# Idle matmuls at the start of a fused attention and softplus kernel: seven instead of ten, and fewer in the gaps behind them

## The chip, the core and the metric

The kernel runs on one core of a Trainium2 chip. Its engines are TensorE (PE; its weight loads are shown as PEld), VectorE (DVE), ScalarE (ACT), GpSimd (POOL) and SyncE (SP), whose queue issues nearly all DMA transfers. Each engine takes its own instructions strictly in the order in which they were written down; semaphores tie the engines together. The metric is device time in microseconds, the median of several runs.

## The reference

```python
# q, k, v: (8, 8, 576, 64); omega: (128, 64); w_in: (512, 2048); w_out: (2048, 512)
def phi(x):                       # of q * scale and of k * scale
    proj = einsum('bhsd,md->bhsm', x, omega)
    h = proj - sum(x * x, axis=-1, keepdims=True) / 2.0
    h = h - max(h, axis=-1, keepdims=True)
    return exp(h) / sqrt(m)
...
kv = einsum('bhsm,bhsd->bhmd', k_p, v)
z = sum(k_p, axis=2)
attn = einsum('bhsm,bhmd->bhsd', q_p, kv) / (einsum('bhsm,bhm->bhs', q_p, z)[..., None] + 1e-06)
...
h = x @ w_in                      # x: attn as (4608, 512)
g = maximum(h, 0.0) + log1p(exp(-abs(h)))
out = g @ w_out
```

## The kernel before

The work is cut by batch (8) and by "quads" of four heads (2 a batch). Tokens of a quad come in units: `xk` and `xq` are the loaded tiles of keys and queries, `k_0_2` in a tile's name is quad 0, unit 2. Only the first batch matters for what follows; its units hold 128 tokens each, so there are ten units of keys (five for each quad) and ten of queries.

One unit of keys goes this way. SP loads it (L463; queries L465). ACT squares its rows (L474) and DVE sums the squares (L481). PE projects it with omega (L491) into two PSUM banks, `ppk_..._0` and `ppk_..._1`, one for each half of the partitions. DVE takes the maxima out of both banks (L541) and folds them into a bias (L548, L553), and ACT writes the exponents (L561), which frees the banks. For keys PE then adds up keys times values into `kt` (L700). For queries (`ppq`, `smq`) PE turns the exponents (`tpq`, L803), multiplies them with the sums `kvs` (L816), and so on. `x` then goes through the feed-forward part: layer 1 into `h` (L1049 to L1051, three products of high and low parts), softplus on ACT and DVE (L1055 to L1072), layer 2 into `acc` (L1109 to L1111). In between ACT, DVE and POOL unpack the weights (`rawi`, `rawo` to `wi`, `wo`, L373 to L394), which are loaded as 16 pairs.

All of it is first written down as a list of works, each with its engines, a planned cost, the works that it comes after, and the buffers that it takes and gives. `in_order` plays this list through with planned clocks and so fixes the order on every engine. Eight PSUM banks (`at`, `h`, `acc`) are given out by it.

The change concerns idle matmuls: `fill` multiplies a 128x128 tile with itself into a PSUM bank that nobody reads. Ten stand in front of everything else (on `idle`, a tile of zeros that DVE sets first). After planning, `with_fill` walks through PE's works, and where the plan leaves PE idle before a work, it writes idle matmuls (on `ident`) into the gap, as many as the constants give:

```python
n = int((t - last - FILL) / 0.2135) if last is not None and t < until else 0
if last is not None and t < DENSE and w.take:
    n += 2
```

`t` is the planned start of the work, `last` the planned end of the one before on PE, `until` is 70 (planned us), and `w.take` says that the work takes a bank. The matmuls go into a bank that is planned to be free all that time, or else into the bank that the work itself takes. On the core they are ordinary matmuls: PE does them before it does the work behind them, whether or not the plan's gap is there.

Of the kernel before, what the change touches and what calls it, by code (L numbers as in the profile page):

```python
# [35 lines left out]
MARGIN = 0.0000  # L36
START = {"SP": 0.75, "ACT": 1.9, "PE": 4.6}
SLOW = 7.19
FILL = 0.3
DENSE = 12  # L40
PATIENCE = {"PE": 0.0000, "DVE": 0.00, "ACT": 0.1822, "POOL": 0.00, "SP": 3.0950}
LEAN = {"DVE": 0.2675, "POOL": 0.1608, "ACT": 0.00}
SPREAD = ((0, 10.51), (17, 12.01))
# [213 lines left out]
def with_fill(out, held, banks, until, emit):  # L257

    last, all_ = None, []
    for i, w in enumerate(out):  # L260
        if w.engine == "PE":
            t = w.end - w.cost
            n = int((t - last - FILL) / 0.2135) if last is not None and t < until else 0
            if last is not None and t < DENSE and w.take:
                n += 2
            names = [
                b for b in banks if all(x1 <= last and g < i or x0 >= t and f >= i for x0, x1, f, g in held.get(b, []))
            ] if n > 0 else []
            names = names or [box[key] for _, box, key in w.take if box[key] in banks]
            if names and n > 0:  # L270
                all_.append((emit, names[0], n))
            last = w.end
        all_.append(w)
    return all_
# [3 lines left out]
def favor_softplus_kernel(ctx, tc, q0, k0, qx, kx, tx, vv, om, wi, wo, out):  # L278
# [11 lines left out]
    at = ctx.enter_context(tc.tile_pool(name="at", bufs=1))  # L290
# [4 lines left out]
    def bank(name, tag):  # L295
        return ps.tile([P, 512], F32, name=name, tag=tag, bufs=1)

    idle = at.tile([P, P], F32, name="idle", tag="x.0", bufs=1)
# [1280 lines left out]
    def fill(tag, n, idle=ident):  # L1579
        t = bank("fill", tag)[:, :P]  # L1580
        for _ in range(n):
            nc.tensor.matmul(t, idle, idle, start=True, stop=True)  # L1582

    with tc.manual_schedule():
        fill("at.0", 10, idle)
        for w in with_fill(*in_order(works, room, AHEAD, MARGIN), room["any"], 70, fill):
            if isinstance(w, tuple):
                w[0](*w[1:])
                continue
            w.emit(w.engine) if len(w.on) > 1 else w.emit()  # L1590
# [99 lines left out]
```

## Time and profile before

| what | value |
|---|---|
| median of 3 runs | 1006.22 us (1006.0 to 1007.1) |
| the profiled execution, own time | 1006.46 us |
| its span, first to last instruction | 1004.7 us |
| busy: PE, DVE, ACT, POOL | 99%, 80%, 67%, 8% of the span |
| mean granted TensorE clock | 0.999 |
| idle matmuls on PE | 45 (10 on `idle`, 35 on `ident`) |

Times within the trace count from the first instruction of the span. Matmuls are pipelined and their ends are modelled, so two that follow each other overlap in a row's duration, and start times say more than ends. A float32 matmul of the idle kind, of L491 or of L700 is two passes, and a row counts passes (x20 is ten matmuls). An engine's idle time stands in brackets before an instruction, with what ended it.

### The profile page before, as it was taken

Reading aid. Unit: us, or ns where it says so; the run is one execution under the profiler, and the core shown is the slowest. Engines: PE = TensorE matmul, PEld = TensorE weight load, DVE = VectorE, ACT = ScalarE, POOL = GpSimd, SP = SyncE. Lnnn points to the kernel's source line nnn. Section 1 sums busy time; section 2 is a strip of 40 time slices with the busy share of each in tenths; the row PEclk is TensorE's granted clock in tenths of the full one; section 3 lists DMA queues with packets and bytes.
Section 4 is the critical chain, followed back from the end, with each engine's and each line's share of the span. In section 5 each row is a group of like instructions: output and inputs, shape, how many; then the busy total and the mean of one; then the engine's idle time right before and its main releaser. Section 6 shows DMA issues by size and latency. Waiting matters only on the chain.

```text
span 1004.7 us, 17142 instructions
## 1 busy us (share of the span) xinstructions
PE 992.0 (99%) x5753; PEld 807.7 (80%) x5753; DVE 805.4 (80%) x2194; ACT 673.7 (67%) x1629; POOL 79.8 (8%) x90
## 2 busy tenths in 40 slices
PE   9999999999999999999999999999999999999998
PEld 8888888787778787887878787878788778788886
DVE  6999997988868787888888897979889846998600
ACT  6999987757677675666675756756576555777600
POOL 0113211000001000100000000100010000001000
PEclk9999999999999999999999999999999999999999
DMA  9963444443252424442343335243534121000011
GB/s 346 373 242 118 146 151 122 134 117 94 96 149 95 134 93 132 137 114 82 115 120 126 91 95 152 95 132 94 133 117 112 64 79 42 1 1 1 1 53 32
DMA packets 64334, 113.81 MB, mean 113 GB/s; under 512 B 18268, under 2 KB 37112, under 8 KB 64248
## 3 DMA queue, kind: packets, MB, share of 16 engines
q1 hardware_dynamic: 64088, 112.60, 36.1%
q8 instruction: 46, 0.75, 0.3%
q14 instruction: 40, 0.33, 0.1%
q10 hardware_dynamic: 160, 0.13, 0.1%
HBM read 85.68 MB, written 27.03 MB: 112 GB/s over the span
## 4 chain that ended last, share of the span: by engine, by line
PE 87%; DVE 6%; ACT 4%; DMA 1%; issue 1%; POOL 0%; DVEq 0%; ACTq 0%; SPq 0%
PE acc L1109 13%; PE acc L1110 12%; PE acc L1111 12%; PE h L1049 10%; PE h L1050 9%; PE h L1051 9%; PE ppk L491 3%; PE kt L655 3%; PE xp L977 3%; PE pb L1384 2%; PE ppq L516 2%; PE pc L1384 2%; PE pa L1384 1%; DMA xq<-qx 1%; PE fill L1582 1%
## 5 line engine op out<-in xcount | busy, mean ns | idle before, releaser
L1109 PE MATMUL acc<-wo,gh 128*128 128x512 f32 x512 | 204.1, 399 | 0.0
L1110 PE MATMUL acc<-wo,gh 128*128 128x512 f32 x512 | 200.2, 391 | 0.0
L1111 PE MATMUL acc<-wo,gl 128*128 128x512 f32 x512 | 199.7, 390 | 0.0
L1049 PE MATMUL h<-xh,wi 128*128 128x512 f32 (+1 forms) x512 | 190.8, 373 | 1.9 <-DVE u L1064 1.1
L1050 PE MATMUL h<-xl,wi 128*128 128x512 f32 (+1 forms) x512 | 186.1, 364 | 0.0
L1051 PE MATMUL h<-xh,wi 128*128 128x512 f32 (+1 forms) x512 | 185.8, 363 | 0.0
L1055 ACT ACTIVATE u<-h 128x512 f32<-128x512 f32 (+1 forms) x128 | 70.1, 547 | 81.4 <-PE h L1051 79.2
L1109 PEld LDWEIGHTS acc<-wo,gh 128*128 128x128 f32 x512 | 96.2, 188 | 24.9 <-issue 6.8
L1049 PEld LDWEIGHTS h<-xh,wi 128*128 128x128 f32 x512 | 96.4, 188 | 23.4 <-DVE u L1064 3.9
L1111 PEld LDWEIGHTS acc<-wo,gl 128*128 128x128 f32 x512 | 96.1, 188 | 21.2 <-DVE gl L1204 0.4
L1110 PEld LDWEIGHTS acc<-wo,gh 128*128 128x128 f32 x512 | 96.5, 188 | 15.9
L1051 PEld LDWEIGHTS h<-xh,wi 128*128 128x128 f32 x512 | 96.4, 188 | 15.4
L1050 PEld LDWEIGHTS h<-xl,wi 128*128 128x128 f32 x512 | 96.6, 189 | 13.5
L1064 DVE SCALAR_TENSOR_TENSOR u<-h,u 128x512 f32<-128x512 f32 (+1 forms) x128 | 79.2, 619 | 32.7 <-ACT u L1061 31.5
L1068 ACT CAST gh<-u 128x512 fp32r<-128x512 f32 (+1 forms) x101 | 57.2, 566 | 46.0 <-PE acc L1110 29.1
L1072 DVE TENSOR_TENSOR gl<-u,gh 128x512 fp32r<-128x512 f32 (+1 forms) x106 | 68.7, 648 | 14.9 <-ACT gh L1068 13.1
L1061 ACT ACTIVATE u<-u 128x512 f32<-128x512 f32 (+1 forms) x128 | 74.2, 580 | 3.9
L1058 ACT ACTIVATE u<-u 128x512 f32<-128x512 f32 (+1 forms) x128 | 74.3, 581 | 3.2
L887 DVE CUSTOM_DVE_ANT_0 junk<-phq,zb 128x128 bf16<-128x128 f32 (+1 forms) x228 | 67.4, 296 | 7.0 <-ACT phq L561 0.4
L538 ACT ACTIVATE phq<-phq,smq 128x128 f32<-128x128 f32 x194 | 59.5, 389 | 10.1 <-DVE smq L553 10.1
L561 ACT ACTIVATE phk<-ppk,smk 128x128 f32<-128x128 f32 x230 | 63.6, 375 | 3.3 <-DVE smk L553 3.1
L541 DVE TENSOR_REDUCE smk<-ppk 128x4 f32<-128x512 f32 (+2 forms) x80 | 46.0, 595 | 24.5 <-PE ppk L491 24.5
(217 smaller groups left out, 1764.2 us busy)
## 6 DMA issues: line engine op xcount, KB each, us to landing
xk<-kx SPq DMA_DIRECT2D x28, 512.0 KB, 3.8
xq<-qx SPq DMA_DIRECT2D x28, 512.0 KB, 3.6
fdq<-flq SPq DMA_DIRECT2D x28, 512.0 KB, 2.8
qq<-fdq SPq DMA_DIRECT2D x112, 128.0 KB, 2.9
rawi<-wi SPq DMA_DIRECT2D x16, 512.0 KB, 6.7
rawo<-wo SPq DMA_DIRECT2D x16, 512.0 KB, 10.1
out<-o SPq DMA_DIRECT2D x32, 256.0 KB, 2.1
v<-vv SPq DMA_DIRECT2D x14, 576.0 KB, 3.7
```

The source lines that it names most:

```text
L887: nc.vector.tensor_tensor_reduce(jk[r, c % jk.shape[1]], ph[r, c], q.zb[r, h], 1.0, 1e-6, ALU.mult, ALU.add, dn[r, 0, c : c + 1])
L1049: nc.tensor.matmul(b["h"], wh, xh[:, cc, t], start=cc == 0, stop=False)
L1050: nc.tensor.matmul(b["h"], wh, xl[:, cc, t], start=False, stop=False)
L1051: nc.tensor.matmul(b["h"], wl, xh[:, cc, t], start=False, stop=cc == NCC - 1)
L1055: nc.scalar.activation(b["u"], b["h"], AF.Abs)
L1058: nc.scalar.activation(b["u"], b["u"], AF.Exp, scale=-1.0)
L1061: nc.scalar.activation(b["u"], b["u"], AF.Ln, bias=1.0)
L1064: nc.vector.scalar_tensor_tensor(b["u"], b["h"], 0.0, b["u"], ALU.max, ALU.add)
L1072: (nc.vector if e == "DVE" else nc.gpsimd).tensor_tensor(b["gl"], b["u"], b["gh"].bitcast(F32), ALU.subtract)
L1109: nc.tensor.matmul(dst, gh, w2[fc][:, 0, c], start=start, stop=False, **kw)
L1110: nc.tensor.matmul(dst, gh, w2[fc][:, 1, c], start=False, stop=False, **kw)
L1111: nc.tensor.matmul(dst, gl, w2[fc][:, 0, c], start=False, stop=stop, **kw)
```

## The change

Seven idle matmuls stand in front instead of ten; the two extra ones ahead of each early work that takes a bank are gone, with the constant `DENSE`; and a planned gap has to be 1.0 us longer than the matmuls put into it, where it was 0.3 us.

```diff
--- before.py
+++ after.py
@@ -36,8 +36,7 @@
 MARGIN = 0.0000
 START = {"SP": 0.75, "ACT": 1.9, "PE": 4.6}
 SLOW = 7.19
-FILL = 0.3
-DENSE = 12
+FILL = 1.0
 PATIENCE = {"PE": 0.0000, "DVE": 0.00, "ACT": 0.1822, "POOL": 0.00, "SP": 3.0950}
 LEAN = {"DVE": 0.2675, "POOL": 0.1608, "ACT": 0.00}
 SPREAD = ((0, 10.51), (17, 12.01))
@@ -261,8 +260,6 @@
         if w.engine == "PE":
             t = w.end - w.cost
             n = int((t - last - FILL) / 0.2135) if last is not None and t < until else 0
-            if last is not None and t < DENSE and w.take:
-                n += 2
             names = [
                 b for b in banks if all(x1 <= last and g < i or x0 >= t and f >= i for x0, x1, f, g in held.get(b, []))
             ] if n > 0 else []
@@ -1582,7 +1579,7 @@
             nc.tensor.matmul(t, idle, idle, start=True, stop=True)
 
     with tc.manual_schedule():
-        fill("at.0", 10, idle)
+        fill("at.0", 7, idle)
         for w in with_fill(*in_order(works, room, AHEAD, MARGIN), room["any"], 70, fill):
             if isinstance(w, tuple):
                 w[0](*w[1:])
```

The plan itself, and with it the order of all other instructions on every engine, is the same. Of the 45 idle matmuls 23 are left: 7 in front, 1 ahead of the fifth group of projections (6 before), none ahead of the second, third and fourth (1 each), the sixth (5) and the first `kt` (2), 15 near 61 us (18) and none near 72 us (1).

The start of PE's queue, before (`ppk` is written by the projection of a unit of keys, four matmuls a group):

```order
L1582 MATMUL fill<-idle 128x128 x10
L491 MATMUL ppk_0_0_0_115<-omf,xk_0_0_106 128x128
L491 MATMUL ppk_0_0_1_116<-omf,xk_0_0_106 128x128
L491 MATMUL ppk_0_0_0_115<-omf,xk_0_0_106 128x128
L491 MATMUL ppk_0_0_1_116<-omf,xk_0_0_106 128x128
L1582 MATMUL fill<-ident 128x128
L491 MATMUL ppk_1_0_0_130<-omf,xk_1_0_108 128x128
L491 MATMUL ppk_1_0_1_131<-omf,xk_1_0_108 128x128
```

And in the changed kernel:

```order
L1579 MATMUL fill<-idle 128x128 x7
L488 MATMUL ppk_0_0_0_112<-omf,xk_0_0_103 128x128
L488 MATMUL ppk_0_0_1_113<-omf,xk_0_0_103 128x128
L488 MATMUL ppk_0_0_0_112<-omf,xk_0_0_103 128x128
L488 MATMUL ppk_0_0_1_113<-omf,xk_0_0_103 128x128
L488 MATMUL ppk_1_0_0_125<-omf,xk_1_0_105 128x128
L488 MATMUL ppk_1_0_1_126<-omf,xk_1_0_105 128x128
L488 MATMUL ppk_1_0_0_125<-omf,xk_1_0_105 128x128
```

Three idle matmuls fewer stand ahead of the first group, and none ahead of the second any more.

What PE does from the fourth group of projections (unit 1 of quad 1) on, before:

```order
L1582 MATMUL fill<-ident 128x128
L491 MATMUL ppk_1_1_0_159<-omf,xk_1_1_112 128x128
L491 MATMUL ppk_1_1_1_160<-omf,xk_1_1_112 128x128
L491 MATMUL ppk_1_1_0_159<-omf,xk_1_1_112 128x128
L491 MATMUL ppk_1_1_1_160<-omf,xk_1_1_112 128x128
L1582 MATMUL fill<-ident 128x128 x6
L491 MATMUL ppk_0_2_0_189<-omf,xk_0_2_123 128x128
L491 MATMUL ppk_0_2_1_190<-omf,xk_0_2_123 128x128
L491 MATMUL ppk_0_2_0_189<-omf,xk_0_2_123 128x128
L491 MATMUL ppk_0_2_1_190<-omf,xk_0_2_123 128x128
L1582 MATMUL fill<-ident 128x128 x5
L491 MATMUL ppk_1_2_0_216<-omf,xk_1_2_137 128x128
```

The same place in the changed kernel (its lines are numbered three lower):

```order
L488 MATMUL ppk_1_1_0_150<-omf,xk_1_1_109 128x128
L488 MATMUL ppk_1_1_1_151<-omf,xk_1_1_109 128x128
L488 MATMUL ppk_1_1_0_150<-omf,xk_1_1_109 128x128
L488 MATMUL ppk_1_1_1_151<-omf,xk_1_1_109 128x128
L1579 MATMUL fill<-ident 128x128
L488 MATMUL ppk_0_2_0_175<-omf,xk_0_2_120 128x128
L488 MATMUL ppk_0_2_1_176<-omf,xk_0_2_120 128x128
L488 MATMUL ppk_0_2_0_175<-omf,xk_0_2_120 128x128
L488 MATMUL ppk_0_2_1_176<-omf,xk_0_2_120 128x128
L488 MATMUL ppk_1_2_0_196<-omf,xk_1_2_132 128x128
```

The six and the five idle matmuls around the fifth group (`ppk_0_2`) are down to one, and the sixth group (`ppk_1_2`) follows the fifth at once.

The second place is near 61 us, between a group of projections of the second batch and layer 1 of the feed-forward part, before:

```order
L491 MATMUL ppk_0_2_0_934<-omf,xk_0_2_868 128x128
L491 MATMUL ppk_0_2_1_935<-omf,xk_0_2_868 128x128
L491 MATMUL ppk_0_2_0_934<-omf,xk_0_2_868 128x128
L491 MATMUL ppk_0_2_1_935<-omf,xk_0_2_868 128x128
L1582 MATMUL fill<-ident 128x128 x18
L1049 MATMUL h_2_1002<-xh,wi_476 128x256
L1050 MATMUL h_2_1002<-xl,wi_476 128x256
```

And in the changed kernel:

```order
L488 MATMUL ppk_0_2_0_911<-omf,xk_0_2_845 128x128
L488 MATMUL ppk_0_2_1_912<-omf,xk_0_2_845 128x128
L488 MATMUL ppk_0_2_0_911<-omf,xk_0_2_845 128x128
L488 MATMUL ppk_0_2_1_912<-omf,xk_0_2_845 128x128
L1579 MATMUL fill<-ident 128x128 x15
L1046 MATMUL h_2_976<-xh,wi_453 128x256
L1047 MATMUL h_2_976<-xl,wi_453 128x256
```

Three idle matmuls fewer stand ahead of the layer-1 group `h_2`; nothing else moved.

## Rows read from the trace of the kernel before

**Rows 1.** The page: part 1 (busy us, share, instructions) and part 4 by engine.
```profile
PE 992.0 (99%) x5753; PEld 807.7 (80%) x5753; DVE 805.4 (80%) x2194; ACT 673.7 (67%) x1629; POOL 79.8 (8%) x90
...
PE 87%; DVE 6%; ACT 4%; DMA 1%; issue 1%; POOL 0%; DVEq 0%; ACTq 0%; SPq 0%
```

**Rows 2.** The chain that ended last, 14 to 110 us: start us, us, what.
```profile
27.82 0.39 ACT kvs L706
...
55.94 0.43 ACT u L1061
56.39 0.42 DVE u L1064
...
102.31 0.42 DVE u L1064
102.77 0.39 PE h L1049
```

**Rows 3.** Timeline of PE, 0 to 30 us: start us, us, instructions.
```profile
1.05 4.64 PE L1582 MATMUL fill<-idle 128*128 128x128 f32 x20 [1.05 <-DVE marks L321]
5.75 1.20 PE L491 MATMUL ppk<-omf,xk 64*128 64x128 f32 x8
...
7.42 0.72 PE L491 MATMUL ppk<-omf,xk 64*128 64x128 f32 x8
...
8.62 0.71 PE L491 MATMUL ppk<-omf,xk 64*128 64x128 f32 x8
...
9.81 0.71 PE L491 MATMUL ppk<-omf,xk 64*128 64x128 f32 x8
10.45 1.60 PE L1582 MATMUL fill<-ident 128*128 128x128 f32 x12
12.12 0.79 PE L491 MATMUL ppk<-omf,xk 64*128 64x128 f32 x8
...
14.27 0.79 PE L491 MATMUL ppk<-omf,xk 64*128 64x128 f32 x8
...
15.75 1.11 PE L700 MATMUL kt<-xk 128*128 128x65 f32 x8
```

**Rows 4.** Timeline of ACT, 4 to 30 us; idle time before in brackets.
```profile
4.54 0.42 ACT L474 ACTIVATE xk<-xk 128x256 f32<-128x256 f32 x1 [2.53 <-DMA xk<-k]
5.55 0.42 ACT L474 ACTIVATE xk<-xk 128x256 f32<-128x256 f32 x1 [0.59 <-DMA xk<-k]
7.15 0.42 ACT L474 ACTIVATE xk<-xk 128x256 f32<-128x256 f32 x1 [1.18 <-DMA xk<-k]
8.47 0.42 ACT L474 ACTIVATE xk<-xk 128x256 f32<-128x256 f32 x1 [0.91 <-DMA xk<-k]
...
11.54 0.62 ACT L561 ACTIVATE xk<-ppk,smk 128x128 f32<-128x128 f32 x2 [0.26 <-DVE smk L553]
...
18.84 1.66 ACT L561 ACTIVATE xk<-ppk,smk 128x128 f32<-128x128 f32 x6 [1.48 <-DVE smk L553]
...
25.46 0.41 ACT L474 ACTIVATE xq<-xq 128x256 f32<-128x256 f32 x1
26.38 1.14 ACT L561 ACTIVATE xq<-ppq,smq 128x128 f32<-128x128 f32 x4 [0.51 <-DVE smq L553]
```

**Rows 5.** Groups by line on DVE, 7 to 27 us: busy, mean | idle before.
```profile
L541 DVE TENSOR_REDUCE smk<-ppk 128x2 f32<-128x256 f32 (+1 forms) x20 | 7.6, 394 | 3.8 <-PE ppk L491 3.8
```

**Rows 6.** Groups by line on ACT, 7 to 27 us.
```profile
L561 ACT ACTIVATE xk<-ppk,smk 128x128 f32<-128x128 f32 x36 | 10.9, 380 | 2.1 <-DVE smk L553 2.1
...
L561 ACT ACTIVATE xq<-ppq,smq 128x128 f32<-128x128 f32 x3 | 0.9, 365 | 0.5 <-DVE smq L553 0.5
```

**Rows 7.** Line 465, the loads of q: from issue to landing.
```profile
DMA to landing us min/median/max: 6.5/6.8/7.2
```

**Rows 8.** Timeline of SP's queue, 16.2 to 16.4 us.
```profile
16.29 0.33 SPq L465 DMA_DIRECT2D xq<-q  x1
```

**Rows 9.** Timeline of PE, 28 to 82 us.
```profile
61.45 4.29 PE L1582 MATMUL fill<-ident 128*128 128x128 f32 x36
```

## The prediction

> **What bounds the kernel now.** I read four views: the page for the whole, the chain of waits for who sets the pace where, and the timelines of PE and ACT for the first 30 us, where the change lies. On the page PE is busy for 99% of the span and makes up 87% of the chain that ended last [rows 1]. That says that time PE gains early can reach the end; it doesn't say that PE sets the pace early. The chain in order of time does: up to about 27 us it runs over PE, from 27.82 to 55.94 us over ACT, from 56.39 to 102.31 us over DVE, and from 102.77 us on over PE, to the end [rows 2]. So what this change does in the first 27 us is worth what it brings ScalarE forward at about 27 us, and no more.
>
> In that stretch the timeline of PE shows the idle matmuls between the groups [rows 3]; that of ACT shows when each load of keys landed, since its squares wait for nothing else: 4.54, 5.55, 7.15, 8.47 us [rows 4]. PE starts the same four groups of projections at 5.75, 7.42, 8.62 and 9.81 us, the fifth and sixth at 12.12 and 14.27, and `kt` at 15.75 us [rows 3]. PE is late, then, by 1.2 us at the first group and 1.9 at the second. The wait passes on: DVE sits idle for 3.8 us ahead of its maxima, because of `ppk` [rows 5], and ACT for 2.1 us and 0.5 us ahead of its exponents, because of the biases that DVE makes of them [rows 6]. The largest of these pauses is 1.48 us at 18.84 us, the last 0.51 us at 26.38 us [rows 4].
>
> **The change part by part.** *Ten to seven in front.* Ten take 4.64 us [rows 3], 0.464 us each, so seven end at 1.05 + 7 x 0.464 = 4.30 us. The first load is there at 4.54 us [rows 4]; the first group then starts at about 4.56 instead of 5.75 us: 1.2 us earlier. It still takes 1.20 us, the slow pace of that time, to 5.76 us.
>
> *None ahead of the second, third and fourth group.* From the third group's start to the fourth's 1.19 us pass, of which the group takes 0.71; one idle matmul and the hand-over behind it cost 0.48 us, and the same before the other two. Without them the second group follows at 5.76 us (its load landed at 5.55), the third waits for its load until 7.15, the fourth until 8.47 us. These groups are bound by loads from here on, so of 3 x 0.48 us only part turns into time: the fourth starts 1.34 us earlier.
>
> *Six to one, five to none, two to none.* Start to start, less the group itself, the six cost 12.12 - 9.81 - 0.71 = 1.60 us, the five 14.27 - 12.12 - 0.79 = 1.36, the two 15.75 - 14.27 - 0.79 = 0.69 [rows 3]. One of them stays, for 0.48. PE alone could now start the fifth group at 8.47 + 0.71 + 0.48 = 9.66, the sixth at 10.45 and `kt` at 11.24 us, 4.5 us earlier than before. But each group takes two of eight PSUM banks, so the fifth and sixth need banks that the exponents of earlier units give back. Exponents that now stand at 11.54 us, behind a pause of 0.26 [rows 4], end at 12.16; half a microsecond earlier they end at 11.7, the rest of the sixth group takes some 0.5, and with hand-overs `kt` starts at about 12.6 us. PE is then 3.1 us ahead (between 2.6, ACT's pauses, and 4.5, PE alone), and stays so, since from 15.75 us on it hardly pauses now.
>
> *What ScalarE makes of it.* Behind the loads of keys, ACT's only idle time up to 27 us is the 2.1 + 0.5 = 2.6 us [rows 6]; the rest is work that the change doesn't touch. If PE is 3.1 us ahead, all of those pauses close, and ACT reaches the head of its chain 2.6 us earlier. It can't go further: the work in between stays, and loads stand next in line. The eighth load of queries is issued at 16.29 us [rows 8] and needs 6.5 to 7.2 us [rows 7], so it lands at 23.5 us at the latest; its square starts at 25.46 us [rows 4], 2.0 us behind, and with the pause of 0.51 us that follows, 2.5 us are to be had before this load shows, 3.2 at its quickest. The bounds of this term are 0 (every pause comes back as a wait for loads) and 3.8 us (DVE's idle time, as if DVE ruled). I take 2.6, since ACT's rows lie on the chain.
>
> *Eighteen to fifteen near 61 us, and the single one behind it.* 36 passes take 4.29 us [rows 9], 0.238 us a matmul: 4 x 0.238 = 0.95 us of PE. The chain there runs over DVE [rows 2], which hides them; if they held DVE up after all, dropping them would bring up to 0.95 us; a loss could come only from the clock, which is a rival below. I take 0.
>
> Behind 27 us ACT, DVE and PE meet the same work in the same order, and the later loads stand in SP's queue behind stores that wait for this work, so they come forward with it. The sum is 2.6 us: for the profiled execution 1006.46 - 2.6 = 1003.9 us. The median is 0.24 us below that execution, so for a median **1003.6 us**, 0.26% less.
>
> **A rule that speaks against it.** The first group takes 1.20 us, the second 0.72 [rows 3]: with the same eight passes, TensorE runs at the lower of its two levels (1.2 and 2.4 GHz) up to some 7 us, and at the higher one behind that. Ahead of the rise it had worked almost without a break since 1.05 us. The mean granted clock of 0.999 (table) has the engine at the higher level afterwards.
>
> The Trainium skill (page TensorE: Matmul & The Clock Gate, section What's actually happening) says that the lower level is the default and that activity lifts it. By that rule idle matmuls earn something, and taking them out may leave the clock low for longer; the trace agrees as far as a rise behind steady work goes, and no row here shows a fall.
>
> **The rivals.** *The clock stays low or falls back, and it gets slower.* After the change PE has pauses between 7 and 12.6 us, waiting for loads, where idle matmuls stood. At the low level it does 0.72 / 1.20 = 0.6 us of work in a microsecond. Up to about 12.6 us this costs nothing, for the loads set the pace there and a group of 1.20 us nearly fits between them. From then on PE loses 0.4 us in each microsecond at the low level. It has 3.1 - 2.6 = 0.5 us to spare over ACT and 2.6 us of gain: these 3.1 us are gone at 12.6 + 3.1 / 0.4 = 20.4 us, and only a clock that is low until then turns the change into a loss. 0.2% or 2.0 us slower takes until 25.4 us. Low until ACT takes over at 27.82 us means 15.2 x 0.4 - 3.1 = 3.0 us more, 1009.2 us. For it: the removed matmuls are 3 x 0.464 + 3 x 0.48 + 1.60 - 0.48 + 1.36 + 0.69 = 6.0 of PE's first 15.75 us. Against it: up to the rise near 7 us PE's work is as unbroken as before but for a few tenths at 4.3 us, and from 12.6 us on nothing lets it pause for long.
>
> *The loads take over.* If the pauses of 0.26 and 0.51 us and part of the large one come back as waits for loads, because ACT's squares stand in its queue ahead of the exponents, some 1.5 us are left: 1004.7 us, with 0.5 to 2.0 us as its bounds (1005.7 to 1004.2). For it: the 2.0 us between the eighth load and its square, less than 2.6. Against: the pause of 0.51 us behind that square.
>
> *It does nothing.* If the idle matmuls only fill gaps that loads make anyway, the time stays 1006.2 us. The first load speaks against it: it lies there for 1.2 us, and DVE's 3.8 us have `ppk` as their cause, not loads.
>
> **How the numbers follow.** The full pull of 2.1 to 3.2 us: 0.66. Loads take over: 0.17. The clock: 0.09. Nothing: 0.08. A difference of 0.2%, 2.0 us, is about what a measurement of this kernel can tell from none. The first case is nearly all beyond that (0.63 of 0.66), and the second adds 0.01: faster 0.64. Slower takes a clock that is low beyond 25 us: 0.06. The rest, 0.30, is the same. The range takes the first two cases, 1003.0 (3.2 us) to 1005.7, and leaves out the last two and a little: 0.18. The first case alone spans 1003.0 to 1004.1 us.
>
> **What would show it.** In the changed profile the six groups of projections should start near 4.6, 5.8, 7.2, 8.5, 9.7 and 10.9 us, and `kt` near 12.6. ACT's idle time ahead of the exponents of keys should fall from 2.1 us to 0.3 or less and that of the first queries from 0.5 to nearly nothing, `kvs` (27.82) should stand near 25.2 us, and the chain should pass from DVE to PE near 100.2 instead of 102.77 us. I am wrong if groups of eight passes take 1.2 us well past 13 us, if ACT has new idle time behind loads of queries or weights, or if the lead of 2.6 us at 27 us is gone again at 103 us.

## The result: slower, with TensorE at its lower level for 34 us

The changed kernel takes 1014.91 us in the median (4 runs, 1011.76 to 1016.29) against 1006.35 for the kernel before beside it (4 runs, 1006.0 to 1007.1): a ratio of 1.0076, with a 95% interval of 1.0054 to 1.0099. That is 8 us slower where 2.6 us faster was forecast. The profiled execution took 1015.46 us with a span of 1013.7 and a mean granted clock of 0.983; before it was 1006.46, 1004.7 and 0.999. A run more than 1.5% above the fastest of its kernel counts in the medians below but not in the ratios (one of b3_ten_singles at 1017.75 us, one of c1_after_four_three at 1023.59 us).

The page of the changed kernel, parts 1 and 4, answers to [rows 1]:

```profile
PE 999.1 (99%) x5709; PEld 815.2 (80%) x5709; DVE 805.5 (79%) x2194; ACT 674.8 (67%) x1629; POOL 79.9 (8%) x90
...
PE 89%; DVE 5%; ACT 3%; DMA 2%; issue 1%; SPq 0%; DVEq 0%; ACTq 0%
```

PE has 44 passes fewer and is busy for 7.1 us more. Work went away and busy time grew, so something got slower for each instruction; DVE's and ACT's busy times are what they were. The timeline of PE says which and where. It answers to [rows 3]: start us, us, instructions, and in brackets the idle time before them.

```profile
1.05 3.35 PE L1579 MATMUL fill<-idle 128*128 128x128 f32 x14 [1.05 <-DVE marks L318]
4.83 1.80 PE L488 MATMUL ppk<-omf,xk 64*128 64x128 f32 x16 [0.43 <-DMA xk<-k]
7.05 0.72 PE L488 MATMUL ppk<-omf,xk 64*128 64x128 f32 x8 [0.42 <-DMA xk<-k]
8.76 0.72 PE L488 MATMUL ppk<-omf,xk 64*128 64x128 f32 x8 [0.99 <-DMA xk<-k]
9.77 0.77 PE L1579 MATMUL fill<-ident 128*128 128x128 f32 x2 [0.29 <-issue]
10.60 2.63 PE L488 MATMUL ppk<-omf,xk 64*128 64x128 f32 x16
13.16 1.97 PE L697 MATMUL kt<-xk 128*128 128x65 f32 x8
15.05 1.23 PE L488 MATMUL ppk<-omf,xk 64*128 64x128 f32 x8
```

Up to the fourth group it is the forecast: groups at 4.83, 7.05 and 8.76 us, bound by loads, for 4.6, 7.2 and 8.5. Then a group of eight passes takes 1.23 us again instead of 0.72, and `kt` 1.97 us where it took 1.11 [rows 3]. The busy time by stretches, with the granted clock, shows how long this lasts. The changed kernel:

```profile
core 0: us, PE busy (x) PEld busy (x) DVE busy (x) ACT busy (x) POOL busy (x), PEclk, DMA share, GB/s
6.20:9.50 3.30, 1.86 (x24) 1.28 (x22) 2.97 (x11) 1.18 (x4) 0.00 (x0) 1.00 0.93 350
9.60:20.00 10.40, 10.17 (x54) 8.93 (x54) 6.71 (x28) 9.45 (x35) 0.41 (x1) 0.50 1.04 402
20.00:30.00 10.00, 10.00 (x50) 8.85 (x51) 6.40 (x25) 5.01 (x17) 0.40 (x1) 0.50 1.04 401
30.00:43.60 13.60, 13.60 (x74) 12.13 (x71) 7.85 (x26) 7.36 (x22) 0.00 (x0) 0.50 0.95 379
43.80:60.00 16.20, 15.21 (x129) 12.99 (x128) 15.45 (x58) 15.74 (x45) 3.83 (x3) 1.00 0.41 136
```

The kernel before, in the same stretches but for the first:

```profile
9.60:20.00 10.40, 10.17 (x92) 8.71 (x90) 7.41 (x31) 8.29 (x31) 0.40 (x1) 1.00 1.04 403
20.00:30.00 10.00, 10.00 (x93) 8.87 (x93) 9.90 (x37) 9.38 (x31) 0.40 (x1) 1.00 1.04 401
```

From 9.6 to 43.6 us the granted clock is 0.50, the lower level; before, it is 1.00 in the same time. Read the row from 20 to 30 us in both: PE is busy for 10.00 of 10.00 us in each, but gets through 93 passes before and 50 in the changed kernel. A busy share can't tell them apart; the clock column can. One caution: the column, and the mean made from it, read 1.00 also ahead of the first record of the clock in a trace (before, the first group takes 1.20 us under a 1.00, and the first record of the higher level is at 6.80 us). Ahead of that record only the time of a known piece of work tells the level: eight passes of `ppk` take 1.2 us at the lower one and 0.72 at the higher. The chain of waits of the changed kernel (start us, us, what) answers to [rows 2]:

```profile
8.76 0.72 PE ppk L488 x8
...
43.28 1.25 PE nuq L813 x8
44.53 0.24 PE xfq L829 x2
44.80 0.37 ACT xh L842
...
66.50 0.42 DVE u L1061
...
113.66 0.39 PE h L1046
```

It stays with PE from 8.76 to 44.77 us; before, ACT has it from 27.82 us on [rows 2]. DVE takes it at 66.50 instead of 56.39 us, and hands it to PE at 113.66 instead of 102.77: 10.9 us late. The idle time that the chain would have to lose first has grown. DVE's groups by line, 7 to 27 us (busy, mean | idle before), answer to [rows 5]: 5.5 us behind `ppk` for 3.8.

```profile
L538 DVE TENSOR_REDUCE smk<-ppk 128x2 f32<-128x256 f32 x15 | 6.0, 417 | 3.2 <-PE ppk L488 3.2
...
L538 DVE TENSOR_REDUCE smk<-ppk 128x1 f32<-128x128 f32 x4 | 1.1, 288 | 2.3 <-PE ppk L488 2.3
```

ACT's groups in the same time answer to [rows 6]: 3.5 us behind the biases for 2.1, and no exponents of queries at all before 27 us.

```profile
L558 ACT ACTIVATE xk<-ppk,smk 128x128 f32<-128x128 f32 x34 | 10.3, 404 | 3.5 <-DVE smk L550 3.5
```

Of the 10.9 us, 1.9 come back later: the spans differ by 9.0. One such place is near 280 us, where the kernel before waits for a load of queries and the changed one, later by then, doesn't. From the chain of the kernel before:

```profile
275.93 5.65 DMA xq<-qx
...
289.77 1.23 PE xp L977 x8
```

and of the changed one, where no load stands in this place and the same `xp` is 8.8 us late:

```profile
298.60 1.23 PE xp L974 x8
```

### The profile page after: what moved, and what is told of

It is laid out like the page before. It is cut to its first block, busy times and chain, and to the rows that moved or that the text cites. A ratio compares the mean times of both kernels' runs of the same rounds, so it can differ in the third digit from the quotient of the medians.

```text
span 1013.7 us, 17049 instructions
## 1 busy us (share of the span) xinstructions
PE 999.1 (99%) x5709; PEld 815.2 (80%) x5709; DVE 805.5 (79%) x2194; ACT 674.8 (67%) x1629; POOL 79.9 (8%) x90
## 4 chain that ended last, share of the span: by engine, by line
PE 89%; DVE 5%; ACT 3%; DMA 2%; issue 1%; SPq 0%; DVEq 0%; ACTq 0%
PE acc L1106 13%; PE acc L1107 12%; PE acc L1108 12%; PE h L1046 10%; PE h L1047 9%; PE h L1048 9%; PE ppk L488 3%; PE kt L652 3%; PE xp L974 3%; PE pb L1381 2%; PE ppq L513 2%; PE pc L1381 2%; PE kt L697 1%; PE pa L1381 1%; PE ppq L488 1%
```

## The experiments

My theory after this: the change loses by the clock, and all else in it does what was forecast. The rivals differ in which of the removed matmuls held the clock. A: the pauses for loads between 6 and 10 us let it fall. B: seven in front are too few to lift it. C: the idle matmuls of 9 to 16 us, ahead of the fifth group, the sixth and `kt`, hold it. Later came D (both the early pauses with seven in front, and the stretch from 10 to 14 us, are to blame), E (only the idle matmuls around the fifth group count) and F (no pause up to the fifth group counts).

The kernels by their idle matmuls: in front, ahead of groups 2 to 4, of the fifth, the sixth, the first `kt`, near 61 us, near 72 us. The ratio is to the kernel before on the same chip, where it took 1006.39 (a), 1006.47 (b) and 1006.73 us (c).

| kernel | front | 2-4 | 5th | 6th | `kt` | 61 | 72 | median us (runs) | ratio, interval |
|---|---|---|---|---|---|---|---|---|---|
| before | 10 | 1,1,1 | 6 | 5 | 2 | 18 | 1 | 1006.35 (4) | 1 |
| after | 7 | 0 | 1 | 0 | 0 | 15 | 0 | 1014.91 (4) | 1.0076, 1.0054 to 1.0099 |
| a1_seven | 7 | 1,1,1 | 6 | 5 | 2 | 18 | 1 | 1003.86 (8) | 0.9984, 0.9963 to 1.0005 |
| a2_no_extra | 10 | 0 | 4 | 3 | 0 | 18 | 1 | 1003.62 (10) | 0.9973, 0.9964 to 0.9983 |
| a3_after_ten | 10 | 0 | 1 | 0 | 0 | 15 | 0 | 1011.74 (5) | 1.0063, 1.0036 to 1.009 |
| a4_burst | 7 | 0 | 1 | 0 | 16 | 15 | 0 | 1007.78 (10) | 1.0016, 1.0006 to 1.0026 |
| b1_seven_no_extra | 7 | 0 | 4 | 3 | 0 | 18 | 1 | 1002.32 (10) | 0.9966, 0.9953 to 0.9978 |
| b2_no_late | 10 | 0 | 4 | 3 | 0 | 0 | 0 | 1002.65 (5) | 0.9965, 0.9952 to 0.9978 |
| b3_ten_singles | 10 | 1,1,1 | 1 | 0 | 0 | 15 | 0 | 1006.31 (10) | 0.9993, 0.9967 to 1.002 |
| b4_one_in_front | 1 | 0 | 4 | 3 | 0 | 18 | 1 | 1003.27 (7) | 0.9967, 0.9956 to 0.9979 |
| c1_after_four_three | 7 | 0 | 4 | 3 | 0 | 15 | 0 | 1002.83 (5) | 0.9965, 0.9951 to 0.9979 |
| c2_after_late_back | 7 | 0 | 1 | 0 | 0 | 18 | 1 | 1011.47 (10) | 1.0057, 1.0028 to 1.0086 |
| c3_after_four | 7 | 0 | 4 | 0 | 0 | 15 | 0 | 1002.87 (5) | 0.9963, 0.995 to 0.9976 |
| c4_front_only | 7 | 0 | 4 | 3 | 0 | 0 | 0 | 1003.57 (6) | 0.9967, 0.9955 to 0.998 |

**a1_seven: the front alone.** Against the kernel before:

```diff
-        fill("at.0", 10, idle)
+        fill("at.0", 7, idle)
```

> The kernel before with seven idle matmuls in front, all others kept. Theory A (the clock falls because PE waits for loads between the second and the fifth group, where the single idle matmuls stood): those pauses stay filled, the clock stays high behind its rise, and the first group starts 1.2 us earlier; 1004.7 us, between 1004.2 and 1006. Rival B (the seven in front are too few, and whatever stands behind them the clock falls): it falls as in the changed kernel, 1012 us or more.

Measured: six of eight runs at 1002.96 to 1006.32 us, two, without a trace, at 1007.91 and 1010.65 (mean clocks of 1.0 and 0.997). In the profiled one (1006.32) the clock first rises at 13.5 us and then stays: groups take 1.22 us up to there, and `kt` starts at 17.87 us at the higher level. So with seven in front the clock can rise later, but by that alone the kernel isn't slower (1003.86 us in the median): B falls as the cause.

**a2_no_extra: the gaps thinned, the front kept.** Against the kernel before:

```diff
-DENSE = 12
+DENSE = 0
```

> The kernel before without the two extra idle matmuls ahead of early works: ten in front, none ahead of the second to fourth group, four, three, none behind (six, five, two before). Theory A: ten in front keep PE behind its loads up to the fourth group, so it hardly pauses between 6 and 10 us, and the clock stays high; 1004 us, between 1003.3 and 1005.5. Rival B: also high. Rival C (each of the idle matmuls between the groups is needed to hold the clock): it falls, 1010 us or more.

Measured: 2.8 us faster, the clock at 1.00 from 7.2 us on. Its chain holds these two lines, which answer to those of [rows 2] at 27.82 and 102.77:

```profile
25.68 0.39 ACT kvs L706
...
100.18 0.39 PE h L1049
```

and ACT's groups by line, 7 to 27 us, answer to [rows 6]:

```profile
L561 ACT ACTIVATE xk<-ppk,smk 128x128 f32<-128x128 f32 x36 | 10.8, 397 | 0.0
...
L561 ACT ACTIVATE xq<-ppq,smq 128x128 f32<-128x128 f32 x5 | 1.5, 365 | 0.0
```

DVE's largest group answers to [rows 5]:

```profile
L541 DVE TENSOR_REDUCE smk<-ppk 128x2 f32<-128x256 f32 x16 | 6.3, 416 | 1.3 <-PE ppk L491 1.3
```

Both of ACT's pauses are gone, and 2.6 us arrive at the hand-over to PE (102.77 to 100.18). This is the forecast gain, in a kernel with fewer idle matmuls whose clock holds.

**a3_after_ten: the changed kernel with ten in front.**

```diff
-        fill("at.0", 7, idle)
+        fill("at.0", 10, idle)
```

> The changed kernel with ten idle matmuls in front instead of seven, so that only the ones behind are fewer. Theory A: PE starts 1.2 us later and finds its first four loads there, so its pauses between 6 and 10 us shrink from 1.5 us to about 0.5; the clock stays high and the time is 1003.8 us, between 1003.2 and 1005. Rival C: the idle matmuls of 9 to 16 us are what held it, so it falls, 1011 to 1016 us. Rival B: high, as in theory A.

Measured: 1011.74 us; no run below 1010.07. By stretches:

```profile
7.20:13.90 6.70, 5.41 (x52) 4.41 (x52) 6.53 (x28) 5.74 (x22) 0.00 (x0) 1.00 1.03 402
14.00:34.30 20.30, 20.30 (x104) 18.02 (x102) 12.55 (x45) 11.56 (x39) 0.80 (x2) 0.50 1.04 401
34.50:60.00 25.50, 24.08 (x213) 20.52 (x213) 24.28 (x88) 25.50 (x71) 3.82 (x3) 1.00 0.56 213
```

The clock outlasts the waits for loads and falls near 14 us, after PE has already begun on `kt`; then it is low for 20 us of unbroken work. A falls in part (the loss comes also with a single wait for a load of 0.27 us there, and ten in front don't prevent it); what is missing lies behind these waits.

**a4_burst: the changed kernel with sixteen idle matmuls ahead of the first `kt`.** `k` counts PE's works:

```diff
-    last, all_ = None, []
+    last, all_, k = None, [], 0
...
+            k += 1
+            n = 16 if k == 7 else n
```

> The changed kernel with sixteen idle matmuls more ahead of the first kt, behind the place where the clock fell. At the low level they take 16 x 0.427 = 6.8 us, from about 13 to 20 us. If dense work of this kind lifts the clock again, it is high from 17 to 21 us on instead of 43.7; PE then stands at kt at about 19 us, some 3 us later than in the kernel before, and all behind follows: 1009 us, between 1007.5 and 1011. If it does not lift the clock, the 6.8 us are added to the changed kernel: 1018 to 1022 us.

Measured: 1007.78 us. The timeline of PE:

```profile
13.04 5.83 PE L1581 MATMUL fill<-ident 128*128 128x128 f32 x32
18.93 1.11 PE L699 MATMUL kt<-xk 128*128 128x65 f32 x8
```

The burst costs PE 5.83 us, and `kt` behind it takes 1.11 us: the records show the rise at 17.25 us, within the burst. In this run the groups ahead of it take 1.2 us each from 4.83 us on, so the clock had not risen at all by then; its mean of 1.000 leaves that time out. (The other nine have mean clocks of 0.995 to 0.998, so a low stretch of a few us, which no trace shows.) A kernel with 5.8 us more of useless work for PE is 7 us faster: C's kind of cause, the clock in the long stretch, and not the work that was moved.

**b1_seven_no_extra: a1 and a2 together** (7 in front, `DENSE = 0`).

> Seven in front, none ahead of the second to fourth group, four and three around the fifth (as in the kernel with ten in front that took 1003.6 us). Theory D (two places each let the clock fall: PE's waits for loads up to 9.6 us when only seven stand in front, and the stretch of 10 to 14 us when fewer than seven stand around the fifth group): up to 9.6 us this kernel is the changed one, so the clock falls there in most runs, and the seven behind it lift it only by chance: 1008 to 1015 us. Rival E (only the idle matmuls around the fifth group count): high throughout, 1003.6 us, between 1002.9 and 1004.7.

Measured: 1002.32 us, the lowest median of the study, though its interval overlaps those of a2, b2 and c3. Its profiled run was the slowest of its ten (1007.52; the others took 1001.26 to 1003.41), and shows what can still happen: low from 8.9 to 15.6 us, so it fell behind the same waits for loads as the changed kernel (PE busy for 1.87 of 3.30 us ahead of the fall, 1.86 there). But here the idle matmuls at 9.58 and 12.91 us follow, and `kt` finds the clock high at 15.78. D is half wrong: the early pauses with seven in front can let it fall, and the idle matmuls behind bring it back ahead of the long stretch. The late return isn't free in this run, though: its chain reaches DVE's `u` at 56.48 us (before 56.39), so the lead is gone, and a load of 7.02 us stands on it at 61.90 us; PE waits 1.82 us for that load, and then the clock is low once more, from 70.3 to 73.7 us, in spite of the eighteen late idle matmuls.

**b2_no_late: a2 without any idle matmuls near 61 and 72 us.**

```diff
-        for w in with_fill(*in_order(works, room, AHEAD, MARGIN), room["any"], 70, fill):
+        for w in with_fill(*in_order(works, room, AHEAD, MARGIN), room["any"], 40, fill):
```

> Ten in front, four and three around the fifth group, and no idle matmuls near 61 and 72 us (eighteen and one before). If DVE's chain hides those, as the prediction has it, the time is that of the same kernel with them, 1003.6 us within 0.4. If they hold up layer 1: up to 0.95 us less, 1002.7 us. If they hold the clock there: a lower mean clock and 1006 us or more.

Measured: 1002.65 us, with intervals that overlap a2's. By stretches:

```profile
62.50:65.80 3.30, 3.30 (x17) 2.85 (x16) 3.30 (x12) 3.30 (x13) 0.00 (x0) 0.50 1.00 393
65.90:80.00 14.10, 14.10 (x142) 12.59 (x140) 13.63 (x33) 13.49 (x34) 2.16 (x2) 1.00 0.58 214
```

In this trace the clock falls for 3.4 us, behind a wait of PE for DVE of 3.61 us, in a place where a2 with the late ones has no fall. PE does set the pace then: the chain runs over it from 61.71 to 77.75 us, where in a2 it stays with DVE. But the cost is small: DVE's `u` starts at 52.99 us here and 53.81 in a2, its `kvs` at 77.75 and 78.28, so 0.3 us of the lead go. In a2 the late ones themselves keep PE until 62.90 us, though DVE's `u` ends at 62.48.

**b3_ten_singles: the changed kernel with ten in front and the singles ahead of groups two to four back.**

```diff
-    last, all_ = None, []
+    last, all_, k = None, [], 0
...
+            k += 1
+            n = 1 if k in (2, 3, 4) else n
...
-        fill("at.0", 7, idle)
+        fill("at.0", 10, idle)
```

> Ten in front, one ahead of the second to fifth group each, none ahead of the sixth and of kt. Theory D: up to 10 us this is the kernel before, but the stretch of 10 to 14 us has one idle matmul instead of thirteen; the clock falls near 14 us as it did with ten in front and no singles, 1010 to 1016 us. Rival F (what counts is that PE has no pause up to the fifth group): high, 1004.5 us, between 1003.5 and 1006.

Measured: runs of two kinds. Five took 1001.33 to 1003.11 us at a mean clock of 0.999 or 1.0, five 1009.5 to 1017.75 at 0.982 to 0.990. The median between them means nothing; in the profiled run (1010.04) the clock is high to 14.4 and low to 34.9 us, as in a3. F comes out wrong: more idle work up to the fourth group doesn't secure a good run. Five of ten are good, against none of five in a3; so few runs don't show that the singles made the difference.

**b4_one_in_front: a2 with a single idle matmul in front.**

```diff
-        fill("at.0", 10, idle)
+        fill("at.0", 1, idle)
```

> One idle matmul in front instead of ten, four and three around the fifth group. Theory D: PE has nothing to do from 1.5 to 4.6 us, so the clock rises at the earliest behind the dense stretch of the fifth and sixth group, or not until 40 us: 1008 to 1018 us. If the idle matmuls in front do nothing: 1003.6 us.

Measured: 1003.27 us, all seven runs between 1001.67 and 1004.47. PE waits for 2.87 us ahead of the first group, and the clock rises only at 13.5 us, behind the idle matmuls around the fifth and sixth group. The front shows no worth for the time.

**c1_after_four_three: the changed kernel with the four and three back, and nothing else.**

```diff
-    last, all_ = None, []
+    last, all_, k = None, [], 0
...
+            k += 1
+            n = {5: 4, 6: 3}.get(k, n)
```

> The changed kernel with four and three idle matmuls ahead of the fifth and the sixth group, where it has one and none; all else as changed (seven in front, none ahead of groups two to four, fifteen near 61 us). If what decides is the idle work around the fifth and sixth group: the clock is high from the middle of that place to the end, and the time is 1001.5 to 1003.5 us, some 12 us under the changed kernel. If the fifteen and the dropped single near 61 and 72 us have a part in it: 1004 us or more.

Measured: four of five runs at 1001.88 to 1004.54 us; one took 1023.59 us, the longest of the study, at a mean clock of 0.972; it wasn't profiled. By stretches, in the run of 1002.83 us:

```profile
4.20:7.50 3.30, 1.93 (x23) 1.45 (x24) 1.33 (x4) 1.23 (x3) 0.00 (x0) 1.00 1.01 384
7.60:10.90 3.30, 3.21 (x21) 2.69 (x18) 3.30 (x16) 2.74 (x10) 0.00 (x0) 0.50 1.03 411
11.00:60.00 49.00, 47.04 (x406) 39.83 (x406) 46.26 (x162) 47.36 (x141) 7.06 (x8) 1.00 0.87 330
```

Here too the clock falls among the waits for loads, at 7.5 us, and comes back at 10.9, after the four idle matmuls of 9.30 us have begun. Six idle matmuls put back into the changed kernel turn 8 us of loss into 3.5 us of gain, in four runs of five.

**c2_after_late_back: the changed kernel with eighteen and one near 61 and 72 us.**

```diff
-    last, all_ = None, []
+    last, all_, k = None, [], 0
...
+            k += 1
+            n = int((t - last - 0.3) / 0.2135) if last is not None and 40 < t < until else n
```

> The changed kernel with the idle matmuls near 61 and 72 us back at eighteen and one. If the place around the fifth and sixth group decides: no help, the clock is low from about 10 to some 35 or 44 us as in the changed kernel, 1010 to 1016 us. If the late ones mattered: nearer to 1006 us or below.

Measured: 1011.47 us; one run of ten at 1002.63 (mean clock 0.999), five at 1010.55 to 1012.12 (0.988), and four at 1016.03 to 1017.29 (0.999 or 1.0). The profiled one (1012.12) has the clock low from 11.5 to 35.2 us. The four have no trace. A clock that is low from the start and rises late would fit them, since the mean leaves that time out, as in a4; it isn't shown. The late ones don't take the loss away: the interval overlaps that of the changed kernel.

**c3_after_four: the changed kernel with four ahead of the fifth group only.** As c1, with `n = 4 if k == 5 else n`.

> The changed kernel with four idle matmuls ahead of the fifth group, and still none ahead of the sixth. If the four alone carry the clock over: 1002 to 1003 us in all runs. If the run of idle work must go on to the sixth group: runs of both kinds, some near 1002 and some with a clock that falls near 10 to 14 us and 1009 to 1016 us.

Measured: all five runs at 1001.45 to 1003.68 us. The timeline of PE in the profiled one:

```profile
7.22 2.40 PE L490 MATMUL ppk<-omf,xk 64*128 64x128 f32 x16 [0.30 <-DMA xk<-k]
9.55 2.07 PE L1581 MATMUL fill<-ident 128*128 128x128 f32 x8
11.68 2.15 PE L490 MATMUL ppk<-omf,xk 64*128 64x128 f32 x16
13.76 1.14 PE L699 MATMUL kt<-xk 128*128 128x65 f32 x8
```

The four don't carry a high clock over here: two groups ahead of them take 2.40 us, the lower level, and the first record of the higher one is at 13.87 us, behind the four and two more groups. From there on it stays high, and `kt` finds it so. Three idle matmuls more than the changed kernel has, in one place, are enough in these runs.

**c4_front_only: b1 without the late ones** (`until` 40 as in b2).

> Seven in front, none ahead of groups two to four, four and three ahead of the fifth and sixth, and none later (near 61 and 72 us). If the late ones are worth nothing, as with ten in front (1002.65 us without them against 1003.62 us with them): 1001 to 1002.5 us, the clock low for a few us near 62 us. If they are worth their time with seven in front: 1003 us or more.

Measured: 1003.57 us, the clock low from 62.9 to 69.7 us. By the bounds that I had set (1001 to 1002.5 us if the late ones are worth nothing, 1003 or more if they are worth their time) it would speak for them. The ratios, 0.9967 here and 0.9966 for b1 with them, don't: as in b2, no worth of the late ones shows.

## Why the prediction was wrong

**The step that failed** is the argument against the rival of the clock: that "from 12.6 us on nothing lets it pause for long", and so the clock would stay. PE didn't pause: it was busy for all of 13.60 us from 30 to 43.6, and the clock stayed low all the same. I took unbroken work for enough to hold or lift the clock. The runs show that it isn't: `kt` and the projections ran on at a high clock (before, a2, c3) and left a low one low for 20 to 34 us (after, a3, b3, c2), while the rise came within, or at most 2.3 us behind, four or more idle matmuls around the fifth group (a1, b1, b4, c1, c3), or sixteen of them ahead of `kt` (a4). So the six, five and two that were costed as 3.2 us of PE to be had were also what put the clock right before the long stretch. c3, and four runs of five of c1, pin it to the place ahead of the fifth group. Counted over the kernels: with one idle matmul there and none between it and `kt` (after, a3, b3, c2) 6 of 29 runs stayed below 1004 us and 23 took 1009.5 or more; with four there and none ahead of groups two to four (a2, b1, b2, b4, c1, c3, c4) 47 of 48 took 1007.52 us or less.

**The rival's price** had the right form and the wrong end. I let the low clock run to 27.82 us at most, since ACT sets the pace from there, and got +3.0 us. But a low clock keeps PE on the chain beyond that point; the hand-over itself moved. With the measured end, (43.7 - 12.6) x 0.4 - 3.1 = 9.3 us, for 9.0 measured between the spans. The slope was low as well (50 passes for 93 is a loss of 0.46 us in each microsecond, not 0.4), which fits the 10.9 us at 113 us better; 1.9 of these came back behind it.

**Ten to seven in front:** the first group came at 4.83 us, not 4.56. In this run the clock rose no later for it: the first record of the higher level is at 6.15 us (before 6.80), and the group at 7.05 us takes 0.72. Right as to the cost. But the rise behind seven isn't sure: of the eight profiled kernels with seven in front, a1, c3 and a4 have their first rise only at 13.5, 13.9 and 17.3 us, while all five with ten have it by 7.2 us. It was no gain by itself, though, since the third and fourth group wait for loads: a2 with ten, b1 with seven and b4 with one have ratios of 0.9973, 0.9966 and 0.9967.

**None ahead of groups two to four:** as forecast, these groups follow the loads (7.05 and 8.76 us). The same waits are where the clock falls in the changed kernel, in b1 and in c1. That a low clock up to 12.6 us costs nothing fits c1, where it came back at 10.9 us; in b1 it came back at 15.7 us, and that run was some 5 us slower than the other nine, in part for the load at 61.90 us.

**ACT's 2.6 us:** right in a2, where the clock is high. There the idle time ahead of both kinds of exponents is 0.0, `kvs` starts at 25.68 (forecast 25.2) and PE takes over at 100.18 us (forecast 100.2); the median is 1003.62, and 1003.6 was forecast. ACT shows only 0.3 us of new waits for loads of queries there, so the rival in which the loads take over didn't happen in a2. With seven in front it did in part: the chain of c1 holds loads of queries from 12.98 to 21.06 us; its median is 1002.83 us all the same.

**Eighteen to fifteen, and the single one behind it:** costed at nothing, and c1, b2 and c4 agree within their intervals.

**The Trainium skill** (page TensorE: Matmul & The Clock Gate, section What's actually happening) has the lower level as the default, which activity lifts. I weighed it and let the rows of before, which hold no fall, decide. The runs agree with the first half (before, the first group takes 1.20 us, at the lower level). That a busy PE is activity enough, as I read it, they contradict: from 20.0 to 43.6 us PE of the changed kernel was busy without a break, and the clock stayed at 0.50.

What stays open: what in the idle matmuls lifts the clock that `kt` and the projections lack. They differ in shape and in how they follow each other, and no run varied either. The low stretches also end without idle matmuls, and what PE did then is a hint. In a3 the rise is at 34.40 us:

```profile
32.24 1.23 PE L692 MATMUL kt<-xk 128*128 128x130 f32 x4
33.27 1.06 PE L800 MATMUL tpq<-ident,xq 128*128 128x128 f32 x4
34.12 1.15 PE L697 MATMUL kt<-xk 128*128 128x65 f32 x8
```

In b3 and c2 it comes behind the same two pieces, at 34.96 and 35.33 us. But in the changed kernel the same `tpq`, at 34.70 us, didn't lift it; the rise at 43.70 us came behind eight more passes of `tpq` from 40.22 us on. So `tpq`, which has the shape of the idle matmuls, stands ahead of all four rises, but not every `tpq` brought one. Also open is why c1 had one run at 1023.59.

## What to carry to other kernels

Before idle matmuls are taken out, find the first long stretch in which PE sets the pace and ask whether the clock is high when it begins; in this kernel those just ahead of it, where loads or buffers break up PE's work, were worth their time, and the others (in front, and near 61 and 72 us) showed none. Price a low clock to the end of the stretch as it will be at half speed, not to the hand-over of the old profile. And read the granted clock beside the busy share, in several runs: a kernel near the edge, as b3, gives both times from the same code. A mean clock near 1.0 clears a run only when its trace shows when the clock first rose.

## What the hardware showed that I had not expected

The same work at the same busy share ran at either level: from 20 to 30 us PE was busy for 10.00 of 10.00 us at a granted clock of 1.00 before and at 0.50 after. Once low, the clock stayed low through 20.3 us (a3) to 34.0 us (after) of such work, and in a4 the rise came within the 5.83 us of sixteen idle matmuls. And the fall didn't come with the longest pauses alone: a3 fell near 14 us, where PE had already begun on `kt`, with 5.41 of the 6.70 us ahead of it busy and no pause above 0.43 us.
